# Transposing the second tile in halves, and a DMA of 128 times 4 bytes over all of Wqkv at the start

## The chip, the cores and the metric

The kernel runs on one core of one Trainium2 chip (trn2). Its time is the device time of one execution in microseconds (us). Each execution also has a span: the time from the first to the last instruction that the profile records.

Engines are named as in the profile: PE is the TensorE matmul, PEld its weight load, DVE the VectorE, ACT the ScalarE, POOL the GpSimd, SP the SyncE, which issues most DMAs. A "q" behind a name is the engine's sequencer or, for SP, a DMA issue.

## The reference, cut to what matters

Two layers, each with an attention block (32 heads, a window of 8 positions at a dilation of 2) and a feed-forward block, on 2048 rows of 1024 bf16 numbers:

```
x = x + attention(layernorm(x), wqkv, wo)
x = x + ffn(layernorm(x), w1, b1, w2, b2)     # gelu
x = x + attention(layernorm(x), wqkv, wo)
x = x + ffn(layernorm(x), w1, b1, w2, b2)
```

Only the first microseconds matter for the change: layernorm of the first 128-row tiles of x, and the first projection with the query columns of wqkv.

## The kernel before: the parts that matter

The kernel goes through four groups of four tiles (512 rows). For the very first group it loads tiles x0 to x3, and the query weights in four pieces of 512 KB, interleaved on SP's queue. I call the pieces 1 to 4.

```
load_x(0, 0, 2)
wq_first = [wpool.tile([P, KD // 2, D], BF16, name="wt") for _ in range(2)]
for k in range(0, KD, 2):
    load_wq_piece(wq_first[k // (KD // 2)], k)      # piece 1, x2, piece 2, x3, piece 3, piece 4
    if k < 4:
        load_x(0, 2 + k // 2, 3 + k // 2)
```

While these land, PE runs 14 warm-up matmuls. Then comes the layernorm of the first tiles:

```
def ln_first():
    ...
    stats(0)                                  # DVE: bn_stats, bn_aggr; ACT: sqrt
    stats(1)
    xn0 = norm(0)                             # DVE: one instruction over 128x1024
    xn1 = norm(1)
    transpose_on_pe(xn0, ..., parts=[act.copy] * 4)
    ps = transpose_bias()                     # PE: b1 into columns
    transpose_on_pe(xn1, ..., parts=[vec.tensor_copy] * 2 + [act.copy] * 2)
    warm_up(2)
    act.copy(b1T[:], ps[:])
    stats(2)
    stats(3)
    ...
```

`transpose_on_pe` makes 8 PE transposes into one PSUM tile and copies the result out in parts. The first projection (`qkv_chunk`) runs over the tiles x0 and x1 alone, piece by piece: 14 matmuls for each piece, so it needs piece 1 first and piece 4 last. The transposes of x2 and x3 are placed among those matmuls.

During the projections of the first group, DVE makes the layernorm of the next two groups (tiles 4 to 11, `ln_early`), and DMAs transpose them.

## Time and profile before

| | before |
|---|---|
| time, median of 3 runs | 1230.68 us (1230.61 to 1230.74) |
| span of the profiled run | 1229.1 us |
| PE busy | 1221.3 us, 99% |
| x0 landed | 3.57 us |
| first projection matmul | 8.95 us |
| last matmul ends | 1226.06 us |

Whole lines of the page of the kernel before: the span, the busy time of each engine with its share and its number of instructions, and the chain that ended last, by engine and then by line.

```profile
span 1229.1 us, 13953 instructions
PE 1221.3 (99%) x5723; PEld 632.7 (51%) x5773; DVE 864.2 (70%) x918; ACT 315.1 (26%) x507; POOL 105.2 (9%) x209
...
PE 99%; DVE 0%; issue 0%; DMA 0%
PE acc L117 99%; DMA x<-in_A_x_dram 0%; DVE stats L92 0%; PE acc L218 0%; DVE xn L92 0%; DVE x L92 0%; DVE mv L92 0%; PE acc L181 0%; DVE rstd L92 0%
```

PE is the bottleneck and it has no slack after the start. So only what happens before 8.95 us, what is added to PE's stream, or a transfer that comes too late can change the time.

The start of the chain of waits, in order of time. The columns are the start in us, the length in us, and what the chain went through.

```profile
0.73 2.85 DMA x<-in_A_x_dram
...
3.60 1.30 DVE stats L92 x2
...
6.58 0.56 DVE xn L92
...
7.19 0.62 PE acc L218 x8
7.81 0.12 PE acc L181
7.92 0.55 PE acc L218 x8
8.48 0.43 PE acc L117 x2
...
8.95 4.12 PE acc L117 x36
```

From x0's landing (0.73 + 2.85 = 3.58) to the projection at 8.95 the chain is 5.4 us long: DVE's statistics and norms, the transposes of tile 0 (7.19), of the bias (7.81) and of tile 1 (7.92), two warm-up matmuls (8.48), then the projection. PE could not transpose tile 1 sooner: DVE makes its norm in one instruction, which starts at 7.24 and ends at 7.79 (start, length, engine, line, operation, output<-inputs, shape, count).

```profile
7.24 0.55 DVE L92 TENSOR_SCALAR xn<-x,mv,rstd 128x1024 bf16<-128x1024 bf16 x1
```

The projection in the timeline of PE, with the same columns: once started, it runs without a gap.

```profile
9.75 3.33 PE L117 MATMUL acc<-xnT,wt 128*128 128x256 bf16 x29
12.91 0.61 PE L218 MATMUL acc<-ident,xn 128*128 128x128 bf16 x8
```

What the core's 16 DMA engines moved in the first 16 us, in slices of 0.4 us (the row of GB/s of the DMA view):

```profile
GB/s 0 0 0 0 20 133 353 359 405 359 260 287 215 161 278 343 394 405 405 395 398 401 410 384 384 405 394 374 379 405 384 369 399 394 379 379 399 389 374 389
```

There is a dip: after 405 in the slice from 3.2 us it falls to 161 in the slice from 5.2 us, and is back at 394 from 6.4 us. By the order of the issues, the packets of that stretch belong to the first transfers behind x1, piece 1 above all (the records do not name the transfer). By the packet records some of them took up to 1.1 us, where 84 ns is usual for 2 KB. This dip is what the touch of the change is aimed at.

### The profile page before, as it was taken

Reading aid. Unit: us, or ns where it says so; the run is one execution under the profiler, and the core shown is the slowest. Engines: PE = TensorE matmul, PEld = TensorE weight load, DVE = VectorE, ACT = ScalarE, POOL = GpSimd, SP = SyncE. Lnnn points to the kernel's source line nnn. Section 1 sums busy time; section 2 is a strip of 40 time slices with the busy share of each in tenths; the row PEclk is TensorE's granted clock in tenths of the full one; section 3 lists DMA queues with packets and bytes.
Section 4 is the critical chain, followed back from the end, with each engine's and each line's share of the span. In section 5 each row is a group of like instructions: output and inputs, shape, how many; then the busy total and the mean of one; then the engine's idle time right before and its main releaser. Section 6 shows DMA issues by size and latency. Waiting matters only on the chain.

```text
span 1229.1 us, 13953 instructions
## 1 busy us (share of the span) xinstructions
PE 1221.3 (99%) x5723; PEld 632.7 (51%) x5773; DVE 864.2 (70%) x918; ACT 315.1 (26%) x507; POOL 105.2 (9%) x209
## 2 busy tenths in 40 slices
PE   9999999999999999999999999999999999999998
PEld 7666544456444564446544465444654444444444
DVE  8999896998997999375993759937599797011001
ACT  4343253014410144202441024410244001400310
POOL 3010015010101101100001000010000002000000
PEclk9999999999999999999999999999999999999999
DMA  9954674756648745856557565576664558446441
GB/s 299 293 205 154 178 238 153 201 171 206 215 133 239 188 151 167 235 169 181 155 160 233 171 171 175 155 222 202 171 199 145 189 195 203 155 160 195 154 136 52
DMA packets 220031, 226.64 MB, mean 184 GB/s; under 512 B 68194, under 2 KB 187136, under 8 KB 217920
## 3 DMA queue, kind: packets, MB, share of 16 engines
q1 hardware_dynamic: 214704, 208.69, 56.9%
q0 software_dynamic: 5264, 17.06, 3.6%
q8 instruction: 45, 0.74, 0.2%
q14 instruction: 18, 0.15, 0.0%
HBM read 189.01 MB, written 4.19 MB: 157 GB/s over the span
## 4 chain that ended last, share of the span: by engine, by line
PE 99%; DVE 0%; issue 0%; DMA 0%
PE acc L117 99%; DMA x<-in_A_x_dram 0%; DVE stats L92 0%; PE acc L218 0%; DVE xn L92 0%; DVE x L92 0%; DVE mv L92 0%; PE acc L181 0%; DVE rstd L92 0%
## 5 line engine op out<-in xcount | busy, mean ns | idle before, releaser
L117 PE MATMUL acc<-xnT,wt 128*128 128x512 bf16 (+1 forms) x3392 | 720.3, 375 | 0.1
L117 PEld LDWEIGHTS <-wt 128*128 128x128 bf16 x3392 | 400.8, 119 | 318.0 <-issue 0.5
L117 PE MATMUL acc<-wt,hT 128*128 128x512 bf16 (+1 forms) x1780 | 386.0, 376 | 2.1
L117 PEld LDWEIGHTS <-hT 128*128 128x128 bf16 x1820 | 178.1, 98 | 209.0
L92 DVE TENSOR_TENSOR big<-big 128x1024 bf16<-128x1024 bf16 (+2 forms) x184 | 244.7, 1358 | 2.2
L92 ACT ACTIVATE hT<-acc,b1T 128x512 bf16<-128x512 f32 x224 | 152.1, 687 | 325.1 <-PE acc L117 325.0
L92 DVE TENSOR_TENSOR big<-qT,kT 128x4096 bf16<-128x4096 bf16 x64 | 143.8, 2284 | 36.4 <-ACT kT L92 35.9
L92 DVE TENSOR_TENSOR tmp<-acc,b2bc 128x512 f32<-128x512 f32 x56 | 38.6, 689 | 161.6 <-PE acc L117 158.5
L92 DVE TENSOR_TENSOR big<-abc,vT 128x4096 bf16<-128x4096 bf16 x64 | 144.6, 2284 | 9.8 <-DMA abc<-a 7.4
L92 ACT CAST qT<-acc 128x512 bf16<-128x512 f32 (+1 forms) x72 | 38.2, 543 | 277.6 <-PE acc L117 277.6
L117 PE MATMUL acc<-wt,oT 128*128 128x512 bf16 x440 | 97.6, 379 | 0.5
L92 DVE BATCH_NORM_STATS2 stats<-x 128x6 f32<-128x512 bf16 x120 | 79.9, 680 | 3.7 <-DMA x<-in_A_x_dram 2.7
L117 PEld LDWEIGHTS <-oT 128*128 128x128 bf16 x448 | 43.8, 98 | 53.0 <-DVE oT L92 0.3
L92 DVE TENSOR_TENSOR x<-acc,big 128x512 bf16<-128x512 f32 (+1 forms) x9 | 5.7, 632 | 90.1 <-PE acc L117 90.0
L92 ACT CAST vT<-acc 128x512 bf16<-128x512 f32 x64 | 37.4, 585 | 100.9 <-PE acc L117 100.8
L92 POOL TENSOR_TENSOR rstd<-mv,eps_t 128x1 f32<-128x1 f32 x56 | 17.4, 311 | 527.5 <-DVE mv L92 527.5
L92 ACT CAST kT<-acc 128x512 bf16<-128x512 f32 x64 | 37.3, 585 | 68.7 <-PE acc L117 68.7
L92 DVE TENSOR_TENSOR x<-acc,x 128x512 bf16<-128x512 f32 x64 | 43.0, 672 | 4.9 <-PE acc L117 4.4
L92 DVE TENSOR_SCALAR xn<-x,mv,rstd 128x1024 bf16<-128x1024 bf16 x52 | 28.4, 546 | 19.9 <-POOL rstd L92 19.5
L92 DVE TENSOR_TENSOR x<-tmp,x 128x512 bf16<-128x512 f32 x56 | 38.6, 689 | 1.4
L92 POOL DMA_DIRECT2D big<-big x24 | 13.3, 563 | 212.8 <-DVE big L92 212.8
L92 POOL TENSOR_TENSOR rstd<-rstd,mhalf 128x1 f32<-128x1 f32 x56 | 30.9, 551 | 4.4
(63 smaller groups left out, 259.4 us busy)
## 6 DMA issues: line engine op xcount, KB each, us to landing
wt<-in_B_w_dram SPq DMA_DIRECT2D x56, 1024.0 KB, 5.8
wt<-in_B_w_dram SPq DMA_DIRECT2D x64, 896.0 KB, 4.9
wt<-in_A_wqkv_dram SPq DMA_DIRECT2D x46, 1024.0 KB, 5.7
wt<-in_A_wo_dram SPq DMA_DIRECT2D x16, 1024.0 KB, 5.3
abc<-a POOLq DMA_DIRECT2D x32, 256.0 KB, 4.7
big<-big POOLq DMA_DIRECT2D x24, 256.0 KB, 3.8
x<-in_A_x_dram SPq DMA_DIRECT2D x16, 256.0 KB, 5.7
out_dram<-x SPq DMA_DIRECT2D x31, 128.0 KB, 1.8
```

Of the source, the lines that this page charges most:

```text
L92: inst = f(*args, **kwargs)
L117: return pe(nc.tensor.matmul(*args, **kwargs))
```

## The change

Its intent has two parts. The first part shortens the start: the norm of the second tile comes in two halves, so that PE can transpose the first half while DVE makes the second; the bias transpose and two warm-up matmuls leave the start. To make room, some work is moved: the statistics of tiles 10 and 11 go from DVE to ACT, their norm and DMA transposes come later (`ln_end`), and the loads of tiles 8 to 11 go behind the key weights. The second part is the touch: a DMA on ACT's queue that reads 4 bytes from each of 128 rows spread over all of Wqkv, in the hope that the slow first accesses to Wqkv are over when the weight pieces are asked for.

The core of the diff (plumbing cut, the comments added here):

```
     load_x(0, 0, 2)
+    touch = lnp.tile([P, 2], BF16, name="less")
+    act.dma_start(touch[:], A_wqkv.rearrange("(p r) f -> p r f", p=P)[:, 0, 0:2])
 ...
         xn0 = norm(0)
-        xn1 = norm(1)
+        xn1 = norm(1, 2)                      # two instructions of 128x512
         transpose_on_pe(xn0, xa[0][:, 0, :, :], parts=[act.copy] * 4)
-        ps = transpose_bias()
-        transpose_on_pe(xn1, xa[0][:, 1, :, :], parts=[vec.tensor_copy] * 2 + [act.copy] * 2)
-        warm_up(2)
-        act.copy(b1T[:], ps[:])
+        transpose_on_pe(xn1, xa[0][:, 1, :, :], parts=[vec.tensor_copy] * 2, k1=KD // 2)
+        transpose_on_pe(xn1, xa[0][:, 1, :, :], parts=[act.copy] * 2, k0=KD // 2)
 ...
         if n == 0:
+            load_x(2)                         # behind the key weights now
             early_tiles = ln_early((1, None), (2, qk_next))
 ...
+        on_act = tiles[-2:]                   # tiles 10 and 11
+        tiles = tiles[:-2]
 ...
+    def ln_end():
+        vec.on = True
+        for tt, (t, xn, xT) in zip((NTT - 2, NTT - 1), ln_rest.pop()):
+            ln_norm(t, mv_ahead[:, tt, :], rstd_ahead[:, tt, :], xn)
+            sp.dma_start_transpose(xT, xn.rearrange("s (k p) -> s k p", p=P))
+        vec.on = False
 ...
-        load_x(2)
-        stage(gen_qkv(0, qk_next=early), sides=at(14, load_b2))
+        stage(gen_qkv(0, qk_next=early), sides=at(8, transpose_bias) + at(9, ln_stats_ahead, 2, NTT - 2)
+              + at(11, ln_end) + at(14, load_b2))
```

More of the change, by code (lines that the diff above doesn't have):

```diff
@@ L181, in transpose_bias @@
         pe(nc.tensor.transpose(ps[:], b1_rows[:], ident[:KF, :KF]))
-        return ps
+        act.copy(b1T[:], ps[:])
     def ln_stats(t, mv=None, rstd=None):
@@ L195, in ln_stats, with ln_stats_ahead @@
         return mv, rstd
-    def ln_stats_ahead(g):
+    def ln_stats_ahead(g, t0=0):
+        act.on = g == 2
         junk = lnp.tile([P, D], BF16, name="xn", bufs=3)
-        for tt in range(NTT):
+        for tt in range(t0, NTT):
             t, mean, var = g * NTT + tt, mv_ahead[:, tt, 0:1], mv_ahead[:, tt, 1:2]
@@ L207, in ln_stats_ahead @@
             pool.tensor_tensor(out=rstd, in0=rstd, in1=mhalf[:], op=ALU.pow)
+        act.on = False
     def ln_norm(t, mv, rstd, xn=None):
@@ L213, in ln_norm, with transpose_on_pe @@
         return xn
-    def transpose_on_pe(xn, out, parts=None):
+    def transpose_on_pe(xn, out, parts=None, k0=0, k1=KD):
         pst = psum.tile([P, KD, P], BF16, name="acc", bufs=8)
-        for k in range(KD):
+        for k in range(k0, k1):
             pe(nc.tensor.transpose(pst[:, k, :], xn[:, k * P:(k + 1) * P], ident[:]))
         parts = parts or [act.copy]
-        n = KD // len(parts)
+        n = (k1 - k0) // len(parts)
         for h, copy in enumerate(parts):
-            copy(out[:, h * n:(h + 1) * n, :], pst[:, h * n:(h + 1) * n, :])
+            ks = slice(k0 + h * n, k0 + (h + 1) * n)
+            copy(out[:, ks, :], pst[:, ks, :])
     last_transpose = [None]
@@ L247, in stats, with norm @@
             act.activation(stds[tt][:], mvs[tt][:, 1:2], ACT.Sqrt, bias=eps_t[:])
-        def norm(tt):
+        def norm(tt, parts=1):
             rstd = lnp.tile([P, 1], F32, name="rstd")
             vec.reciprocal(rstd[:], stds[tt][:])
-            return ln_norm(tt, mvs[tt], rstd)
+            xn = lnp.tile([P, D], BF16, name="xn", bufs=3)
+            for h in range(parts):
+                cols = slice(h * D // parts, (h + 1) * D // parts)
+                vec.tensor_scalar(out=xn[:, cols], in0=x[tt][:, cols], scalar1=mvs[tt][:, 0:1], scalar2=rstd[:],
+                                  op0=ALU.subtract, op1=ALU.mult)
+            return xn
         stats(0)
@@ L580, in ln_early @@
             yield
+        ln_rest.append(on_act)
+    ln_rest = []
+    def ln_end():
[4 more added lines that the diff above has]
+        vec.on = False
     def stage(gen, count=None, sides=()):
@@ L610 @@
         load_x(1)
-        load_x(2)
-        stage(gen_qkv(0, qk_next=early), sides=at(14, load_b2))
+        stage(gen_qkv(0, qk_next=early), sides=at(8, transpose_bias) + at(9, ln_stats_ahead, 2, NTT - 2) + at(11, ln_end) + at(14, load_b2))
         q1 = gen_qkv(1, defer=True, qk_pool=early, mix=NCH // 2)
```

## The prediction

> What bounds it. The page has PE busy 1221.3 of 1229.1 us (99%), clock 1.00; the chain of waits is 98.8% PE matmul. From the first projection matmul (8.95 us) to the last matmul (1226.05) the timeline shows no PE gap over 0.1 us. So the change can only move the start, PE work put into the stream, and a landing that became late.
>
> The start, by the chain: x0 lands at 3.57; DVE statistics of two tiles to 6.52; norm of tile 0, 6.58 to 7.13; its PE transposes from 7.19; tile 1's wait for DVE's norm (7.24 to 7.79), run 7.86 to 8.48; DVE's first copy 8.52 to 8.81; projection at 8.95. The two warm-up matmuls (8.31 to 8.91) only fill that wait.
>
> What the change does there. Tile 1's norm in halves should take about 0.3 us each (estimate: half of 0.55 plus overhead). The first half is ready near 7.55, before PE leaves tile 0's transposes at 7.65. Four transposes into a PSUM tile of their own end near 8.03, not 8.48; DVE's copy near 8.36. ACT's second copy of tile 0 (ends 8.49) becomes an equal gate. Projection near 8.55: 0.4 us gained. The bias transpose cost nothing at the start (PE waited for the norm there); among the key chunks it costs about 0.1 us of a full PE.
>
> Off the chain: statistics of tiles 10 and 11 (1.44 us of DVE each) go to ACT (26% busy); x loads of tiles 8 to 11 go behind the key weights. The second key half lands at 23.86 for use near 24.9: 0.4 us earlier still fits, and it will land several us earlier. First weight pieces land at 6.71, 8.96, 10.81, 12.16, used at 8.95, 10.5, 12.0, 13.9: in time after a 0.4 us shift. Beyond 60 us I expect only the shift.
>
> The touch. Packets over 150 ns cluster at 3.8 to 6.1 us: about 17 on the first weight pieces, up to 1.1 us each, some 9.5 us on 16 engines (0.6 us each); the DMA row dips from 383 to 213 GB/s. The touch asks for these rows first, to take the stalls early. But the weights have over 1 us of slack, so that buys nothing on the chain, and it meets x0, which has none. The Trainium skill, "DMA: Bandwidth & Descriptors", section "Issuing engines are not separate DMA queues", says DMAs of all issuers run on the same 16 engines and interleave; no trace here shows two hardware queues together yet. Eight touch descriptors per engine arrive with x0's first packets (1.8 us), whose first four already take 0.35 to 0.5 us. I expect x0 to land 0.45 us later (0 to 1.2), all of it reaching PE. ACT's table load moves by the issue, about 0.4 us, harmless.
>
> Sum: -0.4 + 0.1 + 0.45 = +0.15, from 1230.68 to about 1230.8 us, range 1230.1 to 1231.6. Faster by over 2%: 0.003; within 2%: 0.99; slower: 0.007.
>
> Right if: x0 lands at 3.8 to 4.2; slow packets gone from 3.8 to 6.1 and found near 1.8 to 3; tile 1's first transposes directly behind tile 0's; projection start minus x0's landing about 5.0, not 5.38; PE gapless after. Wrong if: x0 still lands at 3.57 (then near 1230.4), slow packets stay (the touch warms nothing), or PE waits for weights, kT or PSUM at 20 to 60 us.
>
> What would make it wrong: a touch that holds x0 for over 1 us; ACT's statistics holding PSUM so that PE stalls; a late landing behind the changed order of DMA semaphores.

## The result, and the profile after

| | before | after |
|---|---|---|
| time, median of 6 runs each | 1230.71 us (1230.61 to 1231.29) | 1231.43 us (1230.93 to 1231.94) |
| ratio | | 1.0005, 95% interval 0.9993 to 1.0018 |
| spans of the runs | 1229.1 (profiled) | 1228.8 to 1229.8, median 1229.3 |
| time minus span | 1.74 (profiled) | 2.11 to 2.16 |
| x0 landed | 3.57 us | 3.43 us |
| first projection matmul | 8.95 us | 8.44 us |
| piece 3 landed | 10.81 us | 11.96 us |
| last matmul ends | 1226.06 us | 1226.14 us |

A ratio here is the mean time of one kernel's runs over that of the other's of the same rounds, so it is not quite the ratio of the medians that I quote. The landing times of single transfers, here and below, are read from the trace: a DMA's issue plus its time to landing.

The same lines of the page after, with one new row from the table of DMA queues:

```profile
span 1229.1 us, 14008 instructions
PE 1224.8 (100%) x5771; PEld 632.7 (51%) x5771; DVE 862.1 (70%) x913; ACT 319.2 (26%) x515; POOL 111.0 (9%) x211
...
q10 hardware_dynamic: 144, 0.00, 0.0%
...
PE 99%; DMA 1%; SPq 0%; DVE 0%; issue 0%
PE acc L117 99%; DMA wt<-in_A_wqkv_dram 1%; SPq L92 0%; PE acc L222 0%; DVE x L92 0%; PE acc L183 0%
```

The new queue q10 is ACT's: 144 packets of 4 bytes, 128 for the rows of the touch and 16 more. PE's larger busy sum says nothing here: the traces before and after hold 5723 and 5771 matmul records, and some records can be missing. What has changed is the chain. It no longer begins with x0 but with weights. Four of its pieces in order of time (start, length, what):

```profile
3.62 8.33 DMA wt<-in_A_wqkv_dram
...
12.00 1.09 PE acc L117 x8
...
25.77 0.12 PE acc L183
25.89 1200.27 PE acc L117 x5588
```

The transfer that begins at 3.62 us is piece 3. It lands at 11.95, and PE, which could have used it at about 11.5, goes on at 12.00. At 25.77 is the bias transpose in its new place. The first statistics, which wait for x0, the two half norms of tile 1, the transposes and the projection in the timeline after:

```profile
3.46 1.29 DVE L92 BATCH_NORM_STATS2 stats<-x 128x6 f32<-128x512 bf16 x2 [2.54 <-DMA x<-in_A_x_dram]
...
7.05 1.24 PE L222 MATMUL acc<-ident,xn 128*128 128x128 bf16 x16
7.10 0.74 DVE L92 TENSOR_SCALAR xn<-x,mv,rstd 128x512 bf16<-128x512 bf16 x2
...
8.44 0.85 PE L117 MATMUL acc<-xnT,wt 128*128 128x256 bf16 x6 [0.15 <-DVE xnT L92]
```

and, for a later stretch:

```profile
9.78 2.05 PE L117 MATMUL acc<-xnT,wt 128*128 128x256 bf16 x16
12.00 1.09 PE L117 MATMUL acc<-xnT,wt 128*128 128x256 bf16 x8 [0.17 <-DMA wt<-in_A_wqkv_dram]
12.93 0.61 PE L222 MATMUL acc<-ident,xn 128*128 128x128 bf16 x8
```

So the projection starts 0.51 us sooner (0.37 by the shorter chain, 0.14 because x0 landed sooner in this execution), and the timeline shows it stopped once, before 12.00. The idle time in brackets is 0.17 us; from start to start PE lost more, because a matmul's recorded end is modelled and lies well after the next could start. By starts, the projection's 29th matmul, the first that needs piece 3, began 3.56 us after its first one, against 3.09 us in the kernel before: 0.47 us lost (0.07 of it already at the 15th, which needs piece 2, landed at 10.03). The transposes of tile 2 stand at 12.93 against 12.91 before. All that was gained at the start is gone again.

The DMA row after, again in slices of 0.4 us:

```profile
GB/s 0 0 0 0 72 123 344 349 392 206 205 259 266 273 261 307 358 379 338 382 375 396 418 401 379 399 379 399 410 394 389 394 410 364 384 399 394 369 384 410
```

The dip is still there, from the slice at 3.6 us to the one at 6.0 us. It begins earlier, is flatter, and is no smaller in sum. By the packet records 2.20 MB had been moved by 9 us, against 2.31 MB before.

### The profile page after: what moved, and what is told of

It is laid out like the page before. It is cut to its first block, busy times and chain, and to the rows that moved or that the text cites. A ratio compares the mean times of both kernels' runs of the same rounds, so it can differ in the third digit from the quotient of the medians.

```text
span 1229.1 us, 14008 instructions
## 1 busy us (share of the span) xinstructions
PE 1224.8 (100%) x5771; PEld 632.7 (51%) x5771; DVE 862.1 (70%) x913; ACT 319.2 (26%) x515; POOL 111.0 (9%) x211
## 4 chain that ended last, share of the span: by engine, by line
PE 99%; DMA 1%; SPq 0%; DVE 0%; issue 0%
PE acc L117 99%; DMA wt<-in_A_wqkv_dram 1%; SPq L92 0%; PE acc L222 0%; DVE x L92 0%; PE acc L183 0%
## 5 line engine op out<-in xcount | busy, mean ns | idle before, releaser
L92 DVE TENSOR_SCALAR xn<-x,mv,rstd 128x1024 bf16<-128x1024 bf16 (+1 forms) x53 | 28.6, 541 | 20.2 <-POOL rstd L92 20.1
```

The source lines that it names most:

```text
L92: inst = f(*args, **kwargs)
```

## The experiments

All twelve ran in three jobs of four, in the order of the table: the first two jobs on chip 11, the third (piece2_first, piece2_first_touch, whole_tile, longer_before) on chip 12. The chip of the result above is not recorded, so I compare landings mainly within these jobs. In each job the kernel before ran nine times: medians 1230.83, 1230.77 and 1230.78 us, with medians of span of 1229.1, 1229.0 and 1229.0 us. "Use" is the start of the first matmul that needs a piece. Each row has five runs, and landings of the one that was profiled.

| run | time, median | span: lowest, median, highest | time minus span | pieces 1, 2, 3 landed | projection starts |
|---|---|---|---|---|---|
| no_touch | 1230.96 | 1228.7, 1228.8, 1228.9 | 2.14 | 7.34, 9.42, 11.46 | 8.45 |
| touch_only | 1230.72 | 1228.8, 1228.9, 1229.9 | 1.80 | 7.85, 10.01, 11.94 | 8.98 |
| touch_sp | 1230.71 | 1228.6, 1228.6, 1228.7 | 2.10 | 7.16, 9.40, 11.40 | 8.47 |
| touch_late | 1230.87 | 1228.6, 1228.7, 1229.3 | 2.16 | 7.39, 9.54, 11.50 | 8.47 |
| after_again | 1231.37 | 1228.8, 1229.3, 1229.6 | 2.12 | 8.36, 10.47, 12.47 | 8.62 |
| touch_x0 | 1231.34 | 1228.6, 1229.2, 1229.6 | 2.10 | 7.96, 10.05, 12.08 | 8.47 |
| touch_w1 | 1230.93 | 1228.7, 1228.8, 1229.3 | 2.14 | 7.43, 9.59, 11.53 | 8.55 |
| warm16 | 1230.96 | 1228.7, 1228.9, 1229.4 | 2.11 | 7.87, 10.09, 11.94 | 8.42 |
| piece2_first | 1230.73 | 1228.7, 1228.8, 1229.0 | 1.83 to 2.14 | 8.23, 10.28, 11.47 | 8.45 |
| piece2_first_touch | 1231.03 | 1228.8, 1228.9, 1229.8 | 2.11 | 8.05, 10.14, 11.50 | 8.59 |
| whole_tile | 1230.94 | 1229.0, 1229.1, 1229.1 | 1.84 | 7.38, 9.52, 11.50 | 8.88 |
| longer_before | 1231.29 | 1229.0, 1229.5, 1230.4 | 1.81 | 8.07, 10.13, 12.18 | 8.86 |

Against the kernel before the ratios lie between 0.9998 and 1.0003, each with an interval of about 0.0013 to either side.

The theory after the result (A): the touch, in ACT's queue beside x0, delays the first weight pieces, and a part of the loss lies outside the span. The rival (B): the first pieces land early or late by chance, from one execution to the next.

### no_touch: the change without the touch

```
-    touch = lnp.tile([P, 2], BF16, name="less")
-    act.dma_start(touch[:], A_wqkv.rearrange("(p r) f -> p r f", p=P)[:, 0, 0:2])
```

> The change without the touch. Theory A (the touch itself makes the first weight pieces late and costs time outside the span): pieces 1 to 4 land near 6.7, 9.0, 10.8, 12.2 us as in the kernel before, PE keeps the 0.4 to 0.5 us gained at the start and never waits for wt; span near 1228.7 us; time minus span falls from 2.12 back to 1.74; time near 1230.4, 0.3 under before. Rival B (the stalls of the first weight pieces vary from one execution to the next, whatever the touch): pieces land near 7.8, 10.0, 12.0, 13.3 again, PE waits at 11.8 us, time as the changed kernel's, 1231.4.

The chain of this run, in order of time:

```profile
7.05 0.93 PE acc L220 x12
...
8.01 0.30 DVE xnT L92
...
8.45 4.15 PE acc L117 x36
12.60 0.45 PE acc L220 x8
```

The projection starts at 8.45 and is not stopped: tile 2's transposes come at 12.60 in the chain, against 13.08 before. The last matmul ends at 1225.71 us, 0.35 us before that of the kernel before, and the spans are 1228.7 to 1228.9. That much agrees with A. But the pieces landed at 7.34 to 12.81, between what A and B expected, with piece 3 only 0.08 us ahead of its use (11.54). And the time outside the span stayed at 2.14: that part of A has fallen. The time is therefore not better than before.

### touch_only: the kernel before plus the touch

```
     load_x(0, 0, 2)
+    touch = lnp.tile([P, 2], BF16, name="less")
+    act.dma_start(touch[:], A_wqkv.rearrange("(p r) f -> p r f", p=P)[:, 0, 0:2])
```

> The kernel before plus the touch alone. Theory A: pieces 1.1 us later (7.8, 10.0, 12.0, 13.3) but still just in time, since its projection starts 0.5 us later (8.9 us): span 1229.0 to 1229.2 as before, x0 landing near 3.4 to 3.6, and 0.37 us more outside the span, so time near 1231.1, 0.3 to 0.4 over before. Rival B: landings as before or random, time as before, 1230.7.

The pieces landed as late as A expected (7.85, 10.01, 11.94), and with the later start of this kernel that was just in time. But there is no extra time outside the span: 1.80 against 1.74 for the kernel before in the same job. So ACT's queue is not what costs 0.37 us there. The profiled run, the slowest of the five (span 1229.9), shows another thing: PE waited for the second half of the key weights, which landed at 25.43.

```profile
25.47 1.73 PE L117 MATMUL acc<-xnT,wt 128*128 128x512 bf16 x7 [0.55 <-DMA wt<-in_A_wqkv_dram]
```

### touch_sp: the same touch on SP's queue, behind x0 and x1

```
-    act.dma_start(touch[:], ...)
+    sp.dma_start(touch[:], ...)
```

> The change with the same touch on SP's queue, behind x0 and x1. If the 0.37 us outside the span belong to the second hardware queue, time minus span is 1.74 here; if they belong to the touch's fetches or to the longer program, 2.1 stays. Landings: each later DMA of SP is issued about 0.45 us later; if the touch of cold rows is what delays the pieces they land 1 us or more late and PE waits for wt at 11 to 13 us; if two queues served in turn are the cause, only 0.45 us late. Time 1230.6 to 1231.0.

The span was 1228.6 to 1228.7 in all five runs, the lowest of all and within 0.1 us; although the pieces were issued 0.45 us later, they landed no later than in no_touch. Time minus span is 2.10, so the queue is not the cause of that part, as touch_only already said. The dip is not gone here either: the packets of more than 150 ns between 3 and 8 us sum to 16.9 us over the 16 DMA engines, against 15.5 us in no_touch. I do not claim that this placement helps; five runs 0.1 to 0.2 us below no_touch are suggestive, no more.

### touch_late: the same DMA on ACT's queue, much later

```
+    def load_b2():
+        touch = lnp.tile([P, 2], BF16, name="less")
+        act.dma_start(touch[:], A_wqkv.rearrange("(p r) f -> p r f", p=P)[:, 0, 0:2])
```

> The change with the same 128 x 4 byte DMA on ACT's queue, but issued among the first query copies, near 18 us, when the first four weight pieces are down. If the 0.37 us outside the span come from ACT's queue being in use at all, time minus span is 2.1 here although the touch is late; pieces land as in the kernel before (6.7 to 12.2), no PE wait, span near 1228.7, time near 1230.8. If they come from the touch at the start, 1.74 and time near 1230.4.

The trace shows the DMA issued at 32.59 us, not near 18 as meant; the first weights were down in either case. Landings and start as no_touch, spans too but for one execution of 1229.3, and time minus span 2.16. By itself that would have confirmed the queue as the cause of 2.1, but no_touch has no such DMA and has 2.14.

### after_again, touch_x0, touch_w1: the change once more, and the same DMA over other rows

touch_x0 reads the rows of x0 (which are loaded anyway), touch_w1 reads 128 rows spread over w1 (which nothing needs before 120 us):

```
-    act.dma_start(touch[:], A_wqkv.rearrange("(p r) f -> p r f", p=P)[:, 0, 0:2])
+    act.dma_start(touch[:], x_in[0:P, 0:2])                                            # touch_x0
+    act.dma_start(touch[:], B_w1.rearrange("(p r) f -> p r f", p=P)[:, 0, 0:2])        # touch_w1
```

> The changed kernel once more, beside the others of this batch. Theory A (the touch on ACT's queue holds back the first weight pieces): pieces land near 7.8, 10.0, 12.0, 13.3 us, some 0.5 us later than in the no_touch run (7.34, 9.42, 11.46, 12.81), PE waits for wt near 11.8 us, spans 1229.0 to 1229.8 with a spread. Rival B (another chip, or chance from execution to execution): landings and span as in the no_touch run, 1228.7 to 1228.9.

> The change with the same DMA (128 x 4 bytes, ACT's queue, same place) that reads the rows of x0, which the first load reads anyway: no row of Wqkv is asked for early. If the late pieces come from asking for rows spread over 6 MB at once (A1), pieces land as without a touch (near 7.35) and spans are 1228.7 to 1228.9. If they come from a second hardware queue with 128 small writes in the first microseconds, whatever it reads (A2), pieces land near 7.8 and spans are 1229.1 to 1229.8 as in the changed kernel.

> The same DMA on ACT's queue over 128 rows spread over all of B_w1, which nothing reads before 120 us. A1: as late as with Wqkv's rows or later (pieces 7.8 or more), since the touched rows are as spread but warm nothing that is needed; if touching Wqkv's rows does warm something, the pieces of this run are later than the changed kernel's. A2: the same 7.8. If neither, 7.35 and span 1228.8.

The changed kernel repeats its result: median time 1231.37, median span 1229.3. In the profiled run pieces 2 and 3 both stopped PE:

```profile
10.52 1.75 PE L117 MATMUL acc<-xnT,wt 128*128 128x256 bf16 x14 [0.18 <-DMA wt<-in_A_wqkv_dram]
12.52 1.09 PE L117 MATMUL acc<-xnT,wt 128*128 128x256 bf16 x8 [0.26 <-DMA wt<-in_A_wqkv_dram]
```

touch_x0, which asks for no row of Wqkv, has the same median within 0.1 us, and its piece 3 landed at 12.08. touch_w1, which asks for rows just as spread, landed piece 3 at 11.53 and lost nothing in the profiled run, the fastest of its five; two of the five had spans of 1229.3. As far as one profile and five executions of each can tell, the rows that are touched do not decide it: late pieces came with the rows of x0 as with those of Wqkv, and asking early for rows spread over w1 did not make them late in the one profile. They do not show that touching Wqkv's own rows makes its pieces earlier either.

### warm16: no touch, and PE's program as long as before

```
-    warm_up(14)
+    warm_up(16)
```

> The change without the touch, and with 16 instead of 14 warm-up matmuls at the start, so that PE's program is as long as before the change (the two removed warm-ups are two loads and two matmuls). They end near 7.0 us at the latest, just before the first transposes (7.05), so the span stays 1228.7 to 1228.9. If the 0.37 us outside the span (2.14 here against 1.75 before) hang on the length of PE's program, time minus span falls to 1.75 and the time to 1230.5; if on another engine's program, 2.14 stays.

Time minus span stays at 2.11, so PE's program length is not its cause. The run turned out to be more useful for the other question. It has no touch at all, and yet its profiled run landed piece 3 at 11.94, as late as the changed kernel's 11.96, with a span of 1229.4; piece 3 was used 3.57 us after the start of the projection, again 0.48 us late. Lateness without a touch is therefore shown: B is true at least in part.

### piece2_first and piece2_first_touch: piece 3 ahead of x3

```
-        if k < 4:
-            load_x(0, 2 + k // 2, 3 + k // 2)
+        if k % 4 == 0:                         # piece 1, x2, piece 2, piece 3, x3, piece 4
+            load_x(0, 2 + k // 4, 3 + k // 4)
 ...
-        stats(2)
-        stats(3)
         for tt in range(2, 4):
+            stats(tt)
             first_late.append((norm(tt), xa[0][:, tt, :, :]))
```

piece2_first has no touch, and five more DVE memsets of a spare tile; piece2_first_touch has the touch.

> The change without the touch, with the third weight piece ahead of x3 on SP's queue, and DVE taking the statistics and norm of tile 2 before the statistics of tile 3 (x3 now lands 0.7 us later). If what still holds PE at 11.5 to 12.5 us is the landing of the third piece, it lands near 10.8 to 11.3 here, for use at 11.5, PE has no gap there and all spans are 1228.5 to 1228.8; an execution whose second piece lands after 10.0 keeps that part late. If the loss is anything else, spans stay 1228.7 to 1229.4. Rider: five DVE memsets of a spare tile make DVE's program as long as before the change; if the 0.37 us outside the span hang on DVE's program, time minus span falls from 2.1 to 1.75 (time 1230.4), otherwise 2.1 stays (1230.8).

> The same order of loads, with the touch on ACT's queue. If the touch costs time only through late weight pieces (first three near 7.9, 10.0, 11.3), most of its loss over no_touch, 0.5 us of span, is gone: 1228.6 to 1229.0, the second piece (use 10.0) now the tight one. If it costs elsewhere (x0, ACT), spans stay 1229.1 to 1229.8.

Without the touch the spans were 1228.7 to 1229.0 although the profiled run was one with very late pieces (8.23, 10.28): piece 3 landed at 11.47 there, 1.2 us behind piece 2 where the usual distance is 2.0, and PE lost 0.31 us to piece 2 and none to piece 3. With the touch the median span was 1228.9, where the changed kernel has 1229.3. That agrees with a loss that comes mainly by way of the third piece's landing, as far as five runs from another job, on another chip, can tell. The prediction of the first run's landing (10.8 to 11.3) missed by 0.2 us.

Two surprises came with these runs. In piece2_first, time minus span took two values in the same kernel: 2.14, 1.84, 2.12, 1.83, 1.84. And the profiled run of piece2_first_touch (span 1229.8) waited for the key weights of the next group:

```profile
60.19 2.16 PE L117 MATMUL acc<-xnT,wt 128*128 128x512 bf16 x9 [0.56 <-DMA wt<-in_A_wqkv_dram]
```

SP's queue tells where this comes from. Before the change (start, length of the issues, operation):

```profile
39.28 1.99 SPq L92 DMA_DIRECT2D x<-in_A_x_dram  x4
41.38 10.68 SPq L92 DMA_DIRECT2D wt<-in_A_wqkv_dram  x5
```

and after it:

```profile
39.47 1.72 SPq L92 DMA_DIRECT2D wt<-in_A_wqkv_dram  x3
44.46 8.84 SPq L92 DMA_TRANSPOSE xnT<-qT  x2
53.40 1.08 SPq L92 DMA_DIRECT2D wt<-in_A_wqkv_dram  x2
```

The postponed transposes of tiles 10 and 11 stand on SP's queue ahead of the second half of the next key weights. That half landed at 56.47 us before, at 59.01 after and at 60.14 in the run that waited for it. The changed kernel itself did not wait there in either of its two profiles. It is a new tight spot that the change brings.

### whole_tile: no touch, and tile 1 not in halves

```
-        xn1 = norm(1, 2)
+        xn1 = norm(1)
-        transpose_on_pe(xn1, xa[0][:, 1, :, :], parts=[vec.tensor_copy] * 2, k1=KD // 2)
-        transpose_on_pe(xn1, xa[0][:, 1, :, :], parts=[act.copy] * 2, k0=KD // 2)
+        transpose_on_pe(xn1, xa[0][:, 1, :, :], parts=[vec.tensor_copy] * 2 + [act.copy] * 2)
```

> The change without the touch and without the halves: tile 1's norm in one instruction and its eight transposes into one PSUM tile, as before the change. If the halves make the 0.5 us gained at the start, the projection starts near 5.35 us after x0's landing again (8.8 to 8.95, not 8.45), the weight pieces are then in time even in executions where they land late, and spans are 1229.0 to 1229.2, narrow. If dropping the two warm-ups and the bias transpose made the gain, it starts near 8.45 and spans are as in no_touch, 1228.7 to 1229.4.

The chain of this run:

```profile
7.13 0.62 PE acc L220 x8
...
7.78 0.63 PE acc L220 x8
...
8.44 0.30 DVE xnT L92
...
8.88 4.13 PE acc L117 x36
```

The projection starts 5.36 us after x0's landing, as before the change (5.38); in all ten profiles with halves it was 5.00 or 5.01. So it is the halves that gain 0.35 us (the halved norm and the halved PSUM tile together; the run does not separate them), and dropping the warm-ups and the bias transpose from the start gains 0.02 us. Spans were 1229.0 to 1229.1 in all five runs: with the later start, pieces that land at 9.52 and 11.50 have slack.

### longer_before: the kernel before, with two more POOL and eight more ACT instructions

```
-    pool.memset(eps_t[:], EPS)
+    for _ in range(3):
+        pool.memset(eps_t[:], EPS)
 ...
-    act.activation(one[:], eps_t[:], ACT.Sqrt)
+    for _ in range(9):
+        act.activation(one[:], eps_t[:], ACT.Sqrt)
```

> The kernel before with two more POOL memsets and eight more ACT activations in its first microseconds, where both engines idle: the lengths that POOL's and ACT's programs have after the change. If the 0.37 us outside the span hang on one of these two programs' length, time minus span goes from 1.78 to 2.1; otherwise 1.75 to 1.8 stays. Span as before, 1228.9 to 1230.0.

Time minus span stays at 1.81, so the lengths of POOL's and ACT's programs are not its cause. Its profiled run again shows the old kernel's tight spot: the key weights landed at 26.00 us instead of 23.86, and PE waited.

```profile
26.05 1.30 PE L117 MATMUL acc<-xnT,wt 128*128 128x512 bf16 x5 [0.91 <-DMA wt<-in_A_wqkv_dram]
```

It shows more, for the question of A and B. It has no touch and not the earlier start, and still its piece 3 landed at 12.18, later than in the changed kernel's first profile, and held PE's weight loads (by starts of matmuls, 0.28 us lost):

```profile
12.22 0.86 PEld L117 LDWEIGHTS <-wt 128*128 128x128 bf16 x8 [0.35 <-DMA wt<-in_A_wqkv_dram]
```

The changed order of loads takes the other spot away: in all eleven profiles with the loads of tiles 8 to 11 behind the key weights, these had landed by 23.16 us, and none waited for them; of the three profiles with the old order two waited.

## Why the prediction was right or wrong

The predicted time (1230.8, range 1230.1 to 1231.6) holds the measured 1231.43, and "within 2%" was right. But of the difference it had only +0.15 us where the medians give +0.72. The sum behind it was right in two of its terms and wrong in the third, and one cost was missing.

- **The halves: right.** Predicted: tile 1's first transposes directly behind tile 0's, projection 0.4 us sooner, about 5.0 us after x0's landing instead of 5.38. Measured: all 16 transposes in one stretch from 7.05, and 5.01 us. whole_tile shows that the halves alone make this gain, and no_touch that it reaches the end when the weights are there: last matmul 0.35 us sooner, made of 0.37 by the shorter chain and 0.13 by an earlier x0, less 0.16 for the bias transpose in its new place. DVE's half norms took longer than my estimate of 0.3 us (0.41 each by the trace), but they overlap by 0.08 us.
- **The warm-ups: right.** Dropping the two warm-up matmuls did not slow what follows. The Trainium skill, "TensorE: Matmul & The Clock Gate", section "What's actually happening", says that TensorE starts at half clock and goes to full clock after about 3.4 us of sustained work, at a point that varies from run to run. The traces agree on the two speeds: the first warm-ups start 427 ns apart, and the transposes that follow start 56 ns apart, in both the profile before and the one after; the last of the 14 warm-ups before start 216 ns apart. They do not agree on the time: before, the step came about 4 us after the first warm-up, and in the first profile after all 14 were still slow, the last one 5.5 us after the first; over all fourteen profiles it came from 3.0 to more than 5.5 us after. (The granted clock of the profile reads 1.00 in this stretch too, so it does not tell of this.)
- **The bias transpose: right, size a little low.** Predicted 0.1 us. The chain gives it 0.12. From the start of the projection to the last matmul the five profiles of the changed stream in which no weights held PE took 1217.18 (whole_tile) to 1217.26 us (no_touch), against 1217.10 before, so 0.08 to 0.16.
- **The touch delays x0 by 0.45 us, and all of it reaches PE: wrong.** This is the step that failed. x0 landed at 3.43 in the changed kernel's first profile and at 3.61 in its second. Over the six profiles with an early DMA on ACT's queue it landed at 3.43 to 3.61, mean 3.54; over the eight others (touch_sp among them) at 3.41 to 3.57, mean 3.47. The means differ by 0.07 us, less than either group scatters, so no delay of x0 is shown, and none of the size predicted. The two queues do share the 16 DMA engines: packets of 4 bytes stand among x0's and x1's from 1.9 to 3.1 us, as the section of "DMA: Bandwidth & Descriptors" that the prediction names would have it. But they took 9 ns each by the packet records.
- **The weights have over 1 us of slack, so their lateness costs nothing: wrong.** This is what replaced it in the sum. For piece 3 the slack was 1.23 us, and 0.73 with the projection 0.5 us sooner; and it was read from one profile, in which piece 3 landed at 10.81. Over the other eleven profiles with the same order of loads it landed at 11.40 to 12.47; the one I had was the earliest of all. With the projection 0.5 us sooner, piece 3 is used at about 11.54, and it held PE in four of the eight profiles with the halves and this order (the change twice, touch_x0, warm16). In the changed kernel's first profile it cost 0.47 us, which has about the size that I had put on x0; so the last matmul, 0.09 us later than before, came out near the forecast by luck. In the second profile pieces 2 and 3 together cost 0.8 us.
- **The touch takes the slow packets early: wrong.** I expected them gone from 3.8 to 6.1 us. Packets over 150 ns between 3 and 8 us sum to 12.6 and 16.5 us in the two profiles of the changed kernel, 9.6 before, 15.5 in no_touch and 17.2 in warm16. So they are not gone. Whether the touch makes them fewer is not settled: the lowest sum of all is that of touch_only (6.1), the highest that of longer_before, without a touch (20.4), but touch_w1, which touches no row of Wqkv, has 12.6 like the change itself. No run shows that the touch warms anything.
- **Does the touch do harm? Not settled.** Of 21 executions with an early DMA on ACT's queue in the otherwise changed kernel (the change twice, touch_x0, touch_w1), 15 had a span of 1229.1 us or more; of the 15 with no such DMA (no_touch, touch_late, warm16), 3 had. That speaks for theory A. But the executions are not evenly spread over the jobs, and in the job of touch_x0 and touch_w1 the kernel before also had more late executions (4 of 9 with a span of 1229.5 or more, against 2 of 9 and 1 of 9 in the others). warm16 was as late with no touch, and touch_w1 as early as no_touch with one; longer_before, the old kernel without a touch, landed piece 3 at 12.18; and with the touch on SP's queue none of five executions was late. Theory A holds at most as "more often late"; why the first pieces are early or late at all stays open.
- **Not foreseen: time outside the span.** The time minus the span is 1.72 to 1.85 us in the kernel before, and 2.07 to 2.19 in the changed one: about 0.35 of the 0.7 us between the medians, and the reason why no_touch, with a span 0.3 us shorter, is not faster. It is not ACT's queue (touch_only 1.80, no_touch 2.14), and not the length of PE's, POOL's or ACT's program (warm16, longer_before). Without the halves it is 1.82 to 1.99, median 1.84, and with five more DVE instructions it took both values in one kernel. What sets it is open; the profile does not cover that time.
- **Beyond 60 us only a shift: right in the changed kernel's two profiles**, but piece2_first_touch shows that the moved transposes leave less room at 60 us. It was among the signs that I named for being wrong, without the cause. The second key half was forecast to land several us earlier than 23.86; it landed at 22.45 and 21.98, 1.4 and 1.9 us earlier.

No version here is shown to be faster than the kernel before: the best medians, 1230.71 (touch_sp), 1230.72 (touch_only) and 1230.73 (piece2_first), are the same as its 1230.8 in their jobs. What could be had by span, 0.3 to 0.4 us, was mostly taken back outside it.

## What to carry to other kernels

A slack that is read from one profile is one draw: before spending it, look at the same landing in several executions, above all for the first transfers of a program. When a start is shortened on a kernel whose bottleneck engine has no gaps, the next thing in line is the transfer that was just in time before, so move that one up in the queue together with the change, and look at what stands behind everything that was postponed. And when a difference is below a microsecond, compare spans as well as times, since the part outside the span can change by as much.

## What the Trainium skill lacked or had wrong

- "DMA: Bandwidth & Descriptors" gives bandwidths by size of transfer and a fixed cost, but I found nothing in it on the first accesses of a program. Here the DMA engines reach about 400 GB/s in the slice at 3.2 us (405 before, 392 after) and then run at 161 to 287 GB/s from 4 to 6 us, with 2 KB packets that take up to 1.6 us (84 ns is usual), and in twelve profiles with the same order of loads the third weight piece lands anywhere from 10.81 to 12.47 us.
- "HBM Reference", section "Latency", has 0.2 us on average and 2 us at high load for an HBM access. The slow packets of up to 1.6 us came in these first microseconds, when the engines moved less than they did later at 390 GB/s with packets of mostly 84 to 95 ns; the load alone does not order these two cases.
- "DMA: Bandwidth & Descriptors", section "Issuing engines are not separate DMA queues", agrees with what was seen (two queues interleaved). It gives no number for what a small DMA on a second queue costs one that is under way; here 128 packets of 4 bytes beside x0 and x1 cost x0 nothing that stands out of the scatter (means 3.54 and 3.47 us).
- "TensorE: Matmul & The Clock Gate", section "What's actually happening", has about 3.4 us of sustained work before full clock. Here matmuls of 512 columns went from 427 to 216 ns between 3.0 and more than 5.5 us after the first one, over fourteen profiles.
- "Runtime: NRT & Kernel Launch" lists stages of a launch before and after the kernel, but I found on no page what makes device time outside the recorded instructions change by tenths of a microsecond between near-equal programs or executions of one: 1.72 to 1.85 us here for one kernel, 2.07 to 2.19 for the other, and both values in a third.
